# Half of expert 1 for one more pair of sequences, moved from plain matmuls to a paired period

## The chip, the cores and the metric

One NeuronCore of a Trainium2 chip runs the whole program. The time of a run is what the device takes for one execution, in microseconds (us). TensorE (PE) multiplies matrices, VectorE (DVE), ScalarE (ACT) and GpSimd (POOL) do elementwise work, SyncE (SP) issues most DMAs. Each engine works through its own instructions in order and waits on semaphores for the others.

## The reference

Four sequences of 768 tokens with 8 heads of 48 values go through a gated linear attention; the 3072 x 384 result goes through a mixture of eight experts, each of which sees every token; the weights of the experts come from eight rounds of row and column normalization of a gate.

```python
f = 1.0 / (1.0 + np.exp(-f_logit))
for t in range(S):
    state = f[:, :, t, :, None] * state + einsum('bhd,bhe->bhde', k[:, :, t], v[:, :, t])
    y[:, :, t] = einsum('bhd,bhde->bhe', q[:, :, t], state)
x = y as (3072, 384)
P = np.exp(x @ w_gate - max)
for _ in range(8):
    P /= P.sum(1, keepdims=True) + 1e-09; P /= P.sum(0, keepdims=True) + 1e-09; P *= N / E
for e in range(E):                      # w1[e] 384 x 1024, w2[e] 1024 x 384
    out += P[:, e:e + 1] * (np.maximum(x @ w1[e], 0.0) @ w2[e])
```

## The kernel before, in words

Every product is done in 16-bit halves: an operand is split into a high and a low part (xh, xl; w1h, w1l; hh, hl), and three matmuls (high times high, high times low, low times high) stand for one.

**Units and pairs.** A sequence is cut into two halves of 384 tokens, called units u = 0 to 7; b = u // 2 is the pair (one sequence). There are two ways to do an expert for some tokens. The *plain* way computes hidden features and outputs directly: the hidden part goes to a PSUM bank (hps), ScalarE makes its high part with a Relu (hh), VectorE the low part (hl), then output matmuls (yps) follow, and the result is stored to DRAM (yr to ys) to be weighted and added later. The *paired* way works on a whole pair b, on one half m of the 1024 hidden features, with sums of blocks: 15 block products stand for the first matrix product, 7 for the second. One such (e, m, b) is a *period*; ORDER lists the periods.

**Which part is done how.** Experts 0 and 1 are done the plain way (RAW lists their units), experts 2 to 7 the paired way: 6 x 2 x 4 = 48 periods. For the pairs in HALVED the second half of expert 1's features (m = 1) isn't done plain but in one more period each at the end of ORDER. `plain(e, u)` gives the number of 128-feature slices that a plain unit does: 8, or 4 for expert 1 and such a pair.

**The stages.** (1) Attention, up to about 360 us: 24 items of 128 tokens, in a loop of steps (`g`). An item starts every 8 steps and takes its turn in each step with a few instructions of each engine; after the items' turns a step calls `fill(n)`, which takes n units of plain matmuls from the one stream `raw_pairs`. FILL lists n from a step on. One 384-column matmul counts 1 unit, a 128-column one a third. (2) The balancing of the gate (`balance`, L1166 to L1193), a chain of small VectorE and TensorE instructions in 38 steps; a step takes LEAD = 6.9 units of plain work as cover, first what is left of `raw_pairs`, then the last two units of RAW. When `raw_pairs` is used up, `prepare_w1` starts on the first two weight blocks of the paired way. Sums of pairs 2 and 3 are made in the same steps (HASTE). (3) The periods, of 15 slots each. A slot has six matmuls of 256 columns of the period itself, then one or two turns of `paired`, the second product of an earlier period (126 matmuls of 192 columns per period). EVENTS lists what the other engines do, by slot; weights for the period four ahead are prepared at slots listed in W1AT, W2AT and, for the first period, W1AT0 and W2AT0. The matmuls keep the order in which they are written: `mm` makes each depend on the one before.

**Where a plain unit is done how.** Units 0 to 2 (TILED = 3) go through `moe_tile`, 128 tokens at a time: hidden group g = 0 (four slices, 36 matmuls of 128 columns into one bank), its eviction (L467, L470), group 1 and its eviction, then 24 output matmuls of 384 columns. Tiles follow one another in the stream, expert 0 and expert 1 in turn for units 1 and 2. Units 3 to 7 go through `moe`, all 384 tokens at once: per slice nine matmuls of 384 columns and an eviction (L420, L421), then the outputs. The lines of the profile for matmuls are all L312, the line of `mm`.

Of the kernel before, what the change touches and what calls it, by code (L numbers as in the profile page):

```python
# [26 lines left out]
FT = FF // 128  # L27
# [51 lines left out]
END = 27  # L79
W1AT = (0, 1, 2, 3, 5, 9, 10, 11, 12, 21, 23, 25, 26)  # L80
W1AT0 = (16, 18, 19, 19, 22, 23, 23, 27, 27, 33, 35, 40, 41)
W2AT = (4, 22, 25, 25, 27, 29, 30, 35, 38)
W2AT0 = (0, 1, 1, 3, 3, 5, 5, 5, 7)
W2AT1 = (3, 8, 10, 12, 13, 13, 14, 14, 19)
# [7 lines left out]
CONVAT = (3, 6, 7, 9, 11)  # L92
LAST_EVENTS = {18: (('gs', 'C', 1, 1), ('gs', 'C', 1, 2), ('hl', 'C', 1)), 19: (('gs', 'C', 1, 3), ('gf', 'F', 2), ('gh', 1, 0), ('gh', 1, 1))}
ENDING = '.0.1.01.1..12.1.22..23.23.34343444'
HALVED = (2, 3)
ORDER = [(e, m, b) for e in range(2, NE) for m in range(2) for b in range(B)] + [(1, 1, b) for b in HALVED]
PAIRED = (0, 1, 2)
BY_POOL = (1,)
# [9 lines left out]
TS = CT * C  # L108
ONES = CT * NP * D * 4
LEADS = 23  # L110
FILL = ((0, 11.7), (1, 10.3), (2, 0), (3, 0), (5, 2), (6, 0), (7, 6), (8, 6), (9, 0), (10, 6), (12, 5.3), (15, 5.3), (17, 5.3), (23, 8.7), (30, 8.7), (43, 8.0), (195, 7))
LEAD = 6.9
FIRSTAT = ((0,), (0,), (0, 4), (0, 7), (1, 9), (5, 10))
SECONDAT = ((16, 17), (18, 20), (17, 18), (17, 21), (20, 21), (20, 22), (24, 24), (24, 25))
# [169 lines left out]
def fast(ctx, tc, qkf, vbd, wg, w1, w2, out, flag):  # L284
# [10 lines left out]
    def behind(ins, first):  # L295
        tc.add_manual_dep(
            ins.ins, first.ins.name,
            mybir.DependencyInfo(mybir.DependencyClass.NoSync, mybir.DependencyReason.DATA),
            reason="issue order")
# [3 lines left out]
    def pin(ins):  # L303
        engine = ins.ins.engine
        if fixed[0]:
            if engine in last:
                behind(ins, last[engine])
            last[engine] = ins
        return ins

    def mm(transpose=False, **kw):
        ins = (nc.tensor.transpose if transpose else nc.tensor.matmul)(**kw)  # L312
        if order:
            behind(ins, order[-1])
        order.append(ins)
# [20 lines left out]
    for h in range(2):  # L336
        nc.gpsimd.affine_select(
            out=mask[h * 64:(h + 1) * 64], in_=mask[h * 64:(h + 1) * 64],
# [27 lines left out]
    def xof(u):  # L366
        return [x[:, :, u % 2, :] for x in xt[u // 2]]
# [24 lines left out]
    def bank(shape, name):  # L392
        n = banks[0]
        banks[0] += 1
        return (psn if n % 2 and not late else psm).tile(shape, F32, name=name, tag="m")

    def plain(e, u):
        return FT // 2 if e == 1 and u // 2 in HALVED else FT

# [42 lines left out]
    tiles, put_off, owed = [0], [False], []  # L442

    def moe_tile(e, u, t):
        w1s, w2s = ws[e]
        if (u, t) not in ready:
            raise RuntimeError("an expert is ahead of its tokens")
        xh, xl = xof(u)
        ts = slice(t * 128, t * 128 + 128)
        h = []  # L450
        for g in range(2):
            ps = bank([128, 4, 128], f"hps_{e}_{u}_{t}_{g}")
            n = 0
            for q, x in ((0, xh), (0, xl), (1, xh)):
                for f in range(4 * g, 4 * g + 4):
                    a = w1s[f // 2][q]
                    fs = slice((f % 2) * 128, (f % 2) * 128 + 128)
                    for k in range(KT):
                        mm(out=ps[:, f % 4, :], lhsT=a[:, k, fs], rhs=x[:, k, ts], start=(n == 0), stop=(q == 1 and k == KT - 1), skip_group_check=True)
                        n += 1  # L460
                        if n < 36:
                            yield 1 / 3
            i = tiles[0] % FT
            tiles[0] += 1
            th, tl = (hp.tile([128, 2, 256], F16, name=f"h{q}_{e}_{u}_{t}_{g}", tag=f"k{q}{i // 6}{i % 6 // 3}{i % 3}").rearrange("p c t -> p (c t)") for q in "hl")
            pf = ps.rearrange("p f t -> p (f t)")
            pin(nc.scalar.activation(out=th, in_=pf, func=AF.Relu))  # L467

            def low(tl=tl, pf=pf, th=th):
                pin(nc.vector.scalar_tensor_tensor(out=tl, in0=pf, scalar=0.0, in1=th, op0=ALU.max, op1=ALU.subtract))  # L470

            if put_off[0]:
                owed.append(low)
            else:
                low()
            h.append([v.rearrange("p (f t) -> p f t", t=128) for v in (th, tl)])
            yield 1 / 3
        ps = bank([128, DM], f"yps_{e}_{u}_{t}")
        n = 0
        for f in range(FT):  # L480
            if len(owed) > 1 - f // 4:
                raise RuntimeError("a low part is owed")
            wh, wl = w2s[f // 2]
            hh, hl = (v[:, f % 4, :] for v in h[f // 4])
            for a, b in ((hh, wh), (hh, wl), (hl, wh)):
                mm(out=ps, lhsT=a, rhs=b[:, f % 2, :], start=(n == 0), stop=(n == 3 * FT - 1))
                n += 1
                if n < 3 * FT:
                    yield 1
        yr = rp.tile([128, DM], F32, name=f"yr_{e}_{u}_{t}", tag="yraw", bufs=3)  # L490
        pin(nc.scalar.activation(out=yr, in_=ps, func=AF.Copy))
        nc.sync.dma_start(out=yscr[e][u, t * 128:(t + 1) * 128], in_=yr)
        yield 1
# [447 lines left out]
    def raw_pairs(pairs):  # L941
        for e in range(2):
            for t in range(TT):
                yield from moe_tile(e, 0, t)
        for u in range(1, TILED):
            for t in range(TT):
                for e in range(2):
                    yield from moe_tile(e, u, t)
        for e, u in pairs:
            if u >= TILED:  # L950
                yield from moe(e, u, ws[e])
# [3 lines left out]
    def fill(n):  # L955
        credit[0] += n
        while credit[0] > 0.01:
            cost = next(filler, 0)
            if cost == 0:
                return False  # L960
            credit[0] -= cost or 1
        return True
# [12 lines left out]
    def go_all(g):  # L975
        for gen in loads.pop(g, []):
            next(gen, None)
# [141 lines left out]
    live, g = [it, nxt], 0  # L1119
# [6 lines left out]
    while live or g < max(begin):  # L1126
# [14 lines left out]
        put_off[0] = g < PUTOFF  # L1141
        fill([n for at_, n in FILL if g >= at_][-1])
        go_all(g)
# [59 lines left out]
    def prepare_w1(e, j, cuts=(3, 5, 8)):  # L1203
        raw = raw_weights(e, 1, j)
        yield
        sums = kw.tile([128, 10, 128], F32, name=f"k1s_{e}_{j}", tag="sums", bufs=1)

        def block(v):
            if isinstance(v, str):
                q = int(v[1])  # L1210
                return raw[:, q // 2, 128 * (q % 2):128 * (q % 2) + 128]
            return sums[:, WPOS.index(v), :]

        for part in (WSUMS[i:k] for i, k in zip((0,) + cuts, cuts + (None,))):
            for r, p, op, q in part:
                pin(nc.gpsimd.tensor_tensor(out=block(r), in0=block(p), in1=block(q), op=ALU.add if op == '+' else ALU.subtract))  # L1216
            yield
        pin(nc.vector.tensor_reduce(out=wmx[:, 0, 4 * e + j:4 * e + j + 1], in_=raw.rearrange("p a f -> p (a f)"), axis=AX.X, op=ALU.max, apply_absolute_value=True))
        yield
        wh, wl = (kw.tile([128, PRODUCTS, 128], F16, name=f"k1{n}_{e}_{j}", tag=f"k1{n}") for n in "hl")  # L1220
        halves = ((slice(0, 5), sums[:, 0:5]), (slice(5, 10), sums[:, 5:10]))
        ones = ((slice(10, 12), raw[:, 0:2, 0:128]), (slice(12, 15), raw[:, 0:3, 128:256]))
        for parts in (halves[:1], halves[1:], ones):
            for at_, src in parts:
                pin(nc.scalar.activation(out=wh[:, at_, :], in_=src, func=AF.Copy, scale=W1S))
            yield
        for at_, src in halves + ones:
            pin(nc.vector.scalar_tensor_tensor(out=wl[:, at_, :], in0=src, scalar=W1S, in1=wh[:, at_, :], op0=ALU.mult, op1=ALU.subtract))  # L1228
            if src is ones[1][1]:
                k1[e, j] = wh, wl  # L1230
            yield
# [233 lines left out]
    def at_all(n, slots, gen):  # L1465
        for slot in slots:
            at_slots(n + slot // PRODUCTS, (slot % PRODUCTS,), gen)

    for n, (e, m, b) in enumerate(ORDER):
        part = n % 4  # L1470
        if n - part + 4 < PERIODS and part in (0, 2):
            e2, m2, _ = ORDER[n - part + 4]
            gen = prepare_w1(e2, 2 * m2 + part // 2)
            at_all(n, W1AT if n else W1AT0, gen)
        if n == 0:
# [214 lines left out]
```

## Time and profile before

| | |
|---|---|
| median of 3 runs | 1459.27 us (1458.95 to 1459.32) |
| profiled execution | 1458.97 us, span 1457.2 us |
| TensorE busy | 1435.4 us (99%), 16188 matmuls |
| weight loads | 1267.0 us (87%) |
| VectorE busy | 1241.6 us (85%) |
| ScalarE busy | 1112.2 us (76%) |
| POOL busy | 1092.3 us (75%) |
| granted TensorE clock, mean | 0.997 |

Busy times are unions of an engine's instructions in the profile. A matmul's row runs from its start to the modelled end of its result, which overlaps the next one's row, so the pace of TensorE is read from starts, not from durations. A bracket at the end of a row is the idle time before the instruction and who ended it.

### The profile page before, as it was taken

To read this page: it belongs to the slowest core of one execution; us is meant where nothing else is said; L and a number is where in the kernel's file an instruction comes from. 1 tells how busy PE (TensorE), PEld (TensorE's weight loads), DVE (VectorE), ACT (ScalarE), POOL (GpSimd) and SP (SyncE) were. 2 spreads that over 40 slices of the span, in tenths; PEclk is the share of its full clock that TensorE was granted. 3 is DMA by queue.
4 is the path that set the end of the run, shared out by engine and by line. 5 is a ranking of instruction groups with operands and counts; after the bars stand their busy time and mean duration, and the time that the engine had idled before them with its cause. 6 is when DMAs were issued, how large, how long until landed. Compare 5 with 4: busy or idle time off the path is not lost.

```text
span 1457.2 us, 40795 instructions
## 1 busy us (share of the span) xinstructions
PE 1435.4 (99%) x16188; PEld 1267.0 (87%) x16188; DVE 1241.6 (85%) x2540; ACT 1112.2 (76%) x2492; POOL 1092.3 (75%) x1288
## 2 busy tenths in 40 slices
PE   7999999999999999999999999999999999999997
PEld 5788886666568899999999999999999999999997
DVE  8868878877868998888899898888888889888886
ACT  7767778875547778888888888888777787778874
POOL 3244665675625769999999999999888888888874
PEclk9999999999999999999999999999999999999999
DMA  9245544541111011222211111111000000000201
GB/s 265 84 113 132 120 110 126 124 120 47 65 49 35 24 40 47 56 62 61 61 55 58 49 50 45 41 51 49 23 23 24 23 23 23 13 15 20 77 13 69
DMA packets 82955, 90.54 MB, mean 62 GB/s; under 512 B 50017, under 2 KB 69601, under 8 KB 82754
## 3 DMA queue, kind: packets, MB, share of 16 engines
q1 hardware_dynamic: 82322, 87.25, 21.6%
q8 instruction: 128, 2.10, 0.6%
q14 instruction: 73, 0.60, 0.1%
q10 hardware_dynamic: 432, 0.59, 0.1%
HBM read 64.03 MB, written 14.16 MB: 54 GB/s over the span
## 4 chain that ended last, share of the span: by engine, by line
PE 73%; DVE 3%; ACT 1%; POOL 0%; issue 0%; ACTq 0%; POOLq 0%; DVEq 0%
PE kyps L312 29%; PE kb_A L312 9%; PE kb_B L312 8%; PE kb_D L312 6%; PE kxps L312 5%; PE kb_C L312 4%; PE yps L312 4%; PE hps L312 3%; PE kb_E L312 2%; PE kb_F L312 2%; DVE k1l L1228 0%; DVE kf L1538 0%; DVE kl L1569 0%; POOL k1s L1216 0%; DVE acc L1387 0%
## 5 line engine op out<-in xcount | busy, mean ns | idle before, releaser
L312 PEld LDWEIGHTS <-k1h 128*128 128x128 f16 x3000 | 282.5, 98 | 21.4 <-issue 1.1
L312 PE MATMUL kyps<-k2h,kgl 128*128 128x192 f16 x1188 | 292.3, 246 | 0.6 <-POOL kgl L1564 0.6
L312 PE MATMUL kyps<-k2h,kgh 128*128 128x192 f16 x1188 | 292.3, 246 | 0.1
L312 PE MATMUL kyps<-k2l,kgh 128*128 128x192 f16 x1188 | 292.2, 246 | 0.0
L312 PEld LDWEIGHTS <-kgh 128*128 128x128 f16 x2400 | 220.9, 98 | 7.2 <-issue 0.5
L1564 POOL TENSOR_TENSOR kgl<-kf,kgh 128x512 f16<-128x512 f32 x148 | 198.4, 1341 | 2.1 <-ACT kgh L1561 2.1
L1387 DVE SCALAR_TENSOR_TENSOR yy<-kyps,pes,part 128x192 f32<-128x192 f32 x270 | 111.5, 413 | 92.5 <-PE kyps L312 82.3
L1564 POOL TENSOR_TENSOR kgl<-kr,kgh 128x512 f16<-128x512 f32 x148 | 175.4, 1185 | 9.1 <-PE kyps L312 7.7
L1430 POOL TENSOR_TENSOR acc<-acc,yy 128x384 f32<-128x384 f32 x135 | 134.9, 1000 | 58.4 <-DVE yy L1387 58.4
L312 PEld LDWEIGHTS <-k1l 128*128 128x128 f16 x1500 | 146.8, 98 | 16.9
L312 PEld LDWEIGHTS <-kh 128*128 128x128 f16 x1200 | 112.6, 98 | 7.9 <-issue 1.3
L312 PEld LDWEIGHTS <-kgl 128*128 128x128 f16 x1200 | 117.4, 98 | 0.9 <-POOL kgl L1564 0.8
L312 PEld LDWEIGHTS <-w1h 128*128 128x128 f16 x1248 | 87.9, 98 | 27.1 <-issue 2.1
L312 PE MATMUL yps<-w2h,hl 128*128 128x384 f16 x336 | 110.1, 328 | 1.0 <-DVE hl L470 0.9
L312 PE MATMUL yps<-w2l,hh 128*128 128x384 f16 x336 | 110.0, 328 | 0.6 <-DVE w2l L385 0.6
L312 PE MATMUL yps<-w2h,hh 128*128 128x384 f16 x336 | 110.1, 328 | 0.2 <-ACT hh L420 0.2
L1515 ACT ACTIVATE cp<-kb_A 128x512 f32<-128x512 f32 x150 | 89.8, 599 | 17.5 <-DVE kb_A L1517 15.9
L1541 POOL TENSOR_TENSOR kr<-kr 128x256 f32<-128x256 f32 x100 | 75.6, 756 | 33.5 <-DVE xbl L1029 26.4
L312 PEld LDWEIGHTS <-hh 128*128 128x128 f16 x672 | 65.1, 99 | 37.2 <-issue 1.0
L1384 ACT ACTIVATE kyps<-kyps 128x192 f32<-128x192 f32 x148 | 47.7, 322 | 65.2 <-PE kyps L312 65.1
L1561 ACT ACTIVATE kgh<-kf 128x512 f16<-128x512 f32 x150 | 94.9, 633 | 1.7 <-DVE kf L1538 1.6
L1561 ACT ACTIVATE kgh<-kr 128x512 f16<-128x512 f32 x150 | 94.3, 629 | 0.6 <-DVE kr L1538 0.6
(323 smaller groups left out, 5383.6 us busy)
## 6 DMA issues: line engine op xcount, KB each, us to landing
q<-in_qkf_dram SPq DMA_DIRECT2D x23, 672.0 KB, 5.0
k1r<-in_w_dram SPq DMA_DIRECT2D x26, 384.0 KB, 3.0
k2r<-in_w_dram SPq DMA_DIRECT2D x26, 384.0 KB, 3.0
ys<-yr SPq DMA_DIRECT2D x48, 192.0 KB, 2.4
yb<-ys SPq DMA_DIRECT2D x48, 192.0 KB, 2.4
vr<-in_vbd_dram SPq DMA_DIRECT2D x24, 192.0 KB, 2.5
out_dram<-acc SPq DMA_DIRECT2D x21, 192.0 KB, 1.9
w1r<-in_w_dram SPq DMA_DIRECT2D x8, 384.0 KB, 9.4
```

What stands on the lines that cost most here:

```text
L312: ins = (nc.tensor.transpose if transpose else nc.tensor.matmul)(**kw)
L1384: pin(nc.scalar.activation(out=out, in_=in_, func=AF.Copy, **kw))
L1387: pin(nc.vector.scalar_tensor_tensor(out=y, in0=ps, scalar=p, in1=z, op0=ALU.mult, op1=ALU.add))
L1430: pin(nc.gpsimd.tensor_tensor(out=y, in0=y, in1=z.rearrange("p s d -> p (s d)"), op=ALU.add))
L1515: pin(nc.scalar.activation(out=fresh(ev[2]), in_=bk, func=AF.Copy))
L1541: pin((nc.gpsimd if ev[2] == 'P' else nc.vector).tensor_tensor(out=r[:, 0], in0=r[:, 1], in1=r[:, 0], op=ALU.subtract))
L1561: pin(nc.scalar.activation(out=hs['g', t][0][i], in_=hs['f' if i else 'r', t], func=AF.Copy))
L1564: pin((nc.vector if tag == str(PERIODS - 1) and ev[1] else nc.gpsimd).tensor_tensor(out=hs['g', t][1][i], in0=hs['f' if i else 'r', t], in ...
```

## The change

HALVED becomes (1, 2, 3): for pair 1, too, the second half of expert 1's features is no longer done in the plain units (1, 2) and (1, 3) but in a period (1, 1, 1), the first of the last group; there are 51 periods instead of 50. `moe_tile`, through which unit (1, 2) goes, now honours `plain(e, u)`: a tile with four slices has one hidden group and 12 output matmuls. FILL hands out 0.3 units less per attention step from step 23 on, and 1.0 less from step 195. Six of the thirteen slots in W1AT0 become earlier ones. Since `first` and `final` follow from ORDER, the output of pair 1 is stored in the new period.

```diff
-W1AT0 = (16, 18, 19, 19, 22, 23, 23, 27, 27, 33, 35, 40, 41)
+W1AT0 = (16, 18, 19, 19, 22, 23, 23, 25, 26, 26, 29, 37, 40)
...
-HALVED = (2, 3)
+HALVED = (1, 2, 3)
 ORDER = [(e, m, b) for e in range(2, NE) for m in range(2) for b in range(B)] + [(1, 1, b) for b in HALVED]
...
-FILL = (..., (17, 5.3), (23, 8.7), (30, 8.7), (43, 8.0), (195, 7))
+FILL = (..., (17, 5.3), (23, 8.4), (43, 7.7), (195, 6.0))
...
         h = []
-        for g in range(2):
+        fts = plain(e, u)
+        for g in range(fts // 4):
             ps = bank([128, 4, 128], f"hps_{e}_{u}_{t}_{g}")
...
-        for f in range(FT):
-            if len(owed) > 1 - f // 4:
+        for f in range(fts):
+            if len(owed) > fts // 4 - 1 - f // 4:
                 raise RuntimeError("a low part is owed")
...
-                mm(out=ps, lhsT=a, rhs=b[:, f % 2, :], start=(n == 0), stop=(n == 3 * FT - 1))
+                mm(out=ps, lhsT=a, rhs=b[:, f % 2, :], start=(n == 0), stop=(n == 3 * fts - 1))
                 n += 1
-                if n < 3 * FT:
+                if n < 3 * fts:
                     yield 1
```

## Rows read from the trace of the kernel before

**Rows 1.** Stretches: each engine's busy us (instructions), granted clock, DMA
```profile
100.00:350.00 250.00, 249.42 (x3621) 188.00 (x3620) 200.60 (x384) 189.63 (x409) 146.17 (x158) 1.00 0.46 114
260.00:280.00 20.00, 19.69 (x286) 13.99 (x284) 18.85 (x35) 16.37 (x37) 11.03 (x13) 1.00 0.58 149
361.00:410.00 49.00, 48.17 (x304) 29.28 (x301) 42.14 (x93) 23.45 (x48) 33.24 (x51) 1.00 0.21 68
380.00:400.00 20.00, 19.47 (x124) 11.74 (x122) 19.09 (x42) 11.48 (x25) 14.58 (x21) 1.00 0.08 30
410.00:425.00 15.00, 15.00 (x95) 8.98 (x92) 5.43 (x10) 6.19 (x12) 0.00 (x0) 1.00 0.12 40
425.00:505.00 80.00, 78.61 (x766) 69.68 (x765) 68.88 (x138) 59.11 (x133) 46.67 (x62) 1.00 0.11 33
560.00:1380.00 820.00, 819.94 (x8759) 778.46 (x8757) 723.54 (x1513) 664.52 (x1528) 732.59 (x856) 1.00 0.14 40
```

**Rows 2.** TensorE in order of time, 86 to 90 us: start, duration, operation
```profile
86.46 0.33 PE L312 MATMUL yps<-w2h,hh 128*128 128x384 f16 x1
86.62 0.33 PE L312 MATMUL yps<-w2l,hh 128*128 128x384 f16 x1
...
89.56 0.34 PE L312 MATMUL yps<-w2h,hl 128*128 128x384 f16 x1 [0.66 <-DVE hl L470]
```

**Rows 3.** All engines in order of time, 186 to 190 us
```profile
186.12 0.83 PE L312 MATMUL hps<-xh,w1h 128*128 128x128 f16 x12
...
187.10 0.60 ACT L467 ACTIVATE hh<-hps 128x512 f16<-128x512 f32 x1
...
187.73 0.69 DVE L470 SCALAR_TENSOR_TENSOR hl<-hps,hh 128x512 f16<-128x512 f32 x1 [1.50 <-ACT hh L467]
...
188.13 0.33 PE L312 MATMUL yps<-w2h,hh 128*128 128x384 f16 x1
...
188.33 0.60 ACT L467 ACTIVATE hh<-hps 128x512 f16<-128x512 f32 x1
...
189.20 0.68 DVE L470 SCALAR_TENSOR_TENSOR hl<-hps,hh 128x512 f16<-128x512 f32 x1
```

**Rows 4.** Tile kb_F, 560 to 1380 us: durations, first and last start
```profile
L1520 DVE TENSOR_TENSOR kb_F<-kb_D,cp x40: 698/699/700, 579.7 to 1368.2; 128x512 f32<-128x512 f32 x40
```

**Rows 5.** All engines in order of time, 137 to 138 us
```profile
137.03 0.33 PE L312 MATMUL yps<-w2h,hh 128*128 128x384 f16 x1
...
137.22 0.60 ACT L467 ACTIVATE hh<-hps 128x512 f16<-128x512 f32 x1 [0.46 <-PE hps L312]
...
137.85 0.69 DVE L470 SCALAR_TENSOR_TENSOR hl<-hps,hh 128x512 f16<-128x512 f32 x1 [1.05 <-ACT hh L467]
```

**Rows 6.** All engines in order of time, 197 to 200 us
```profile
197.64 0.33 PE L312 MATMUL yps<-w2h,hh 128*128 128x384 f16 x1
...
198.96 0.60 ACT L467 ACTIVATE hh<-hps 128x512 f16<-128x512 f32 x1
...
199.11 0.32 PE L312 MATMUL yps<-w2l,hh 128*128 128x384 f16 x1
...
199.59 0.69 DVE L470 SCALAR_TENSOR_TENSOR hl<-hps,hh 128x512 f16<-128x512 f32 x1 [2.03 <-ACT hh L467]
```

**Rows 7.** VectorE in order of time, 86 to 90 us
```profile
88.84 0.66 DVE L470 SCALAR_TENSOR_TENSOR hl<-hps,hh 128x512 f16<-128x512 f32 x1
```

**Rows 8.** VectorE's groups, 410 to 425 us: busy, mean ns, idle before
```profile
L421 DVE SCALAR_TENSOR_TENSOR hl<-hps,hh 128x384 f16<-128x384 f32 x7 | 3.9, 557 | 7.5 <-ACT hh L420 7.4
```

**Rows 9.** All engines in order of time, 393 to 395 us
```profile
394.06 0.30 PEld L312 LDWEIGHTS sk_c<-sk_cs,onesf 128*128 128x128 f32 x2 [0.84 <-DVE sk_cs L1188]
...
394.09 0.72 POOL L1005 TENSOR_TENSOR xs<-x 128x256 f32<-128x256 f32 x1
```

**Rows 10.** VectorE's groups of instructions, 100 to 350 us
```profile
L1029 DVE TENSOR_TENSOR xal<-xs,xah 128x768 f16<-128x768 f32 x3 | 2.9, 951 | 0.0
```

**Rows 11.** VectorE's groups of instructions, 355 to 425 us
```profile
L1029 DVE TENSOR_TENSOR xal<-xs,xah 128x768 f16<-128x768 f32 x6 | 6.9, 1146 | 0.0
```

More of the change, by code (lines that the diff above doesn't have):

```diff
@@ L110 @@
 LEADS = 23
-FILL = ((0, 11.7), (1, 10.3), (2, 0), (3, 0), (5, 2), (6, 0), (7, 6), (8, 6), (9, 0), (10, 6), (12, 5.3), (15, 5.3), (17, 5.3), (23, 8.7), (30, 8.7), (43, 8.0), (195, 7))
+FILL = ((0, 11.7), (1, 10.3), (2, 0), (3, 0), (5, 2), (6, 0), (7, 6), (8, 6), (9, 0), (10, 6), (12, 5.3), (15, 5.3), (17, 5.3), (23, 8.4), (43, 7.7), (195, 6.0))
 LEAD = 6.9
```

## The prediction, made before the changed kernel was built or run

> **What bounds the kernel now.** I read the busy times of each engine by stretch first [rows 1]. TensorE is busy 249.42 of 250 us while attention runs, 48.17 of 49 around the balancing, 819.94 of 820 in the steady part of the paired periods, and the granted clock is 1.00 (2.4 GHz) in all of them. Since overlapping matmuls make a busy TensorE easy to overrate, I checked that it is at its pace: in the list of instructions two output matmuls of 384 columns start 0.16 us apart (86.46 and 86.62, 0.162 over longer runs), and a hidden group of 36 matmuls of 128 columns takes the 2.01 us from 186.12 to 188.13, 0.056 each [rows 2, 3]. So from 100 us on nearly every microsecond of matmul taken away or added counts, and so does every wait on TensorE. VectorE is the next engine: 200.6 of 250 us, 42.1 of 49 [rows 1].
>
> **What goes.** Units (1,2) and (1,3), expert 1 on the two halves of sequence pair 1, lose half of their hidden features. Unit (1,2) is done in 128-token tiles: per tile 36 matmuls of 128 columns and 12 of 384 go, for three tiles 108 x 0.056 + 36 x 0.162 = 11.9 us. Unit (1,3) is done whole: 4 x 9 + 3 x 12 = 72 of 384 columns, 11.7 us. Together 23.6 us, or 144 of the "units" that FILL counts (a unit is one 384-column matmul or three of 128). Seven evictions on ScalarE and seven on VectorE go too; no output store goes.
>
> **What comes.** One more period, (1,1,1): 90 matmuls of 256 columns and 126 of 192. Its length is read from one event per period: 40 of them start between 579.7 and 1368.2 us, 788.5 / 39 = 20.22 us [rows 4]. Weights for (1,1) are prepared for the last group anyway, so it brings no loads, and VectorE, busy 88% in the steady periods with such loads beside [rows 1], has room. The output of pair 1 is stored three periods later, still two periods ahead of the end. Matmul work alone: 20.22 - 23.6 = -3.4 us.
>
> **The step that I think decides: the half tile has nothing to hide its eviction.** A full tile computes hidden group 0, then group 1, then the outputs, which begin with group 0. Group 0's high part (ScalarE) and low part (VectorE) are made beside group 1's 36 matmuls (2.0 us), and group 1's beside the first 12 output matmuls (1.95 us). A half tile has one group: its first output matmul needs the high part and its third the low part at once. Nothing else stands between, since the tiles follow one another in one stream and TensorE keeps the written order.
>
> How long the two parts take, counted from where the next matmul could start: in a quiet tile the next one starts at 137.03, the high part ends at 137.82 and the low part at 138.54: 0.79 and 1.51 us [rows 5]. Behind other work it is 197.64, 199.56 and 200.28: 1.92 and 2.64 [rows 6]; at 186.12 (still hidden of group 1 next) 1.58 and 2.30, and at 188.13 0.80 and 1.75 [rows 3]. One tile shows the wait itself. Its group 1 ends at 86.46 and the low part at 89.50, 3.04 later [rows 7]; the fifteenth output matmul, which needs it, would be due 14 x 0.162 = 2.27 us after 86.46, at 88.73, and starts at 89.56 [rows 2]. So TensorE starts 0.06 after the low part ends and loses what is over. For the half tile the third matmul would be due after 2 x 0.162 = 0.32 us, so a tile loses (low part's end) + 0.06 - 0.32: at least 1.25 us (from 1.51), at most 2.78 (from 3.04).
>
> Which value, from the place in the attention schedule: FILL's new amounts hand out 106.3 units before step 23, 168 in the next 20 steps, then 7.7 a step. The three half tiles finish their hidden part at units 636, 708 and 780, which is late in step 89, early in step 99 and past the middle of step 108. An item starts every 8 steps and issues its score and state matmuls in steps that are 3 above a multiple of 8, its output matmuls in 1, its gate in 7. Step 90 issues none, and 99 and 108 end later than the tile's third matmul, so none of the three waits is covered by attention matmuls (as the one after 197.64 is, whose next output matmul comes at 199.11 in any case [rows 6]). Step 89 has the second scan and the products before it on VectorE: between 1.51 and 2.30, I take 1.9. Step 99 is of the kind of the 186.12 tile but a little earlier in its step: 2.5. Step 108 is of the kind of 188.13 (1.75), 2.5 units or 0.4 us earlier: 2.1. Sum 6.5 - 3 x 0.26 = 5.7 us lost; ends 3.75 and 8.3.
>
> **The smaller terms.** Unit (1,3) and the other half units have this only mildly, since four evictions are spread over 36 matmuls and the last one's low part is due only 11 x 0.162 = 1.78 us later: nothing is lost behind a quiet VectorE (1.51), 0.9 with 2.64. I take 0.2.
> Attention steps get 0.3 units shorter (the last ones 1.0), 65.6 units or 10.7 us in all. VectorE then has about the same work in 240 us for 250, 84% for 80%. In the 20 us from 260 it already has 18.85, and TensorE idles 0.31 there [rows 1]. Nothing lost at the one end, five such stretches at the other, 1.5; I take 0.2.
> The balancing of the gate is 38 steps long and takes 6.9 units a step as cover. Left over for it are 1728 - 1594.3 = 133.7 units before and 1584 - 1528.7 = 55.3 after, plus 216 of the last two units in both: 349.7 or 271.3, against 38 x 6.9 = 262. So the cover still reaches, with little over. But the first two weight blocks, which are prepared once the earlier units are used up, then begin at step 9 instead of 20 and are done before the balancing ends: VectorE gets the 1.5 us of their low parts that now lie after 410 (5.43 us of work there [rows 1], less 3.9 of hidden low parts [rows 8]), and two hidden evictions more (1.1 us), 44.7 for 42.1 us in a stretch of 49 [rows 1]. There TensorE's queue already waits 0.84 us for VectorE's column sums at 394.06 [rows 9]. If VectorE can be 95% busy, as in 380 to 400 (19.09 of 20), nothing is lost; if no more than its 86% there, 44.7 / 0.86 - 49 = 3.0 us. I take 1.2, between the two.
> W1AT0 moves six of the thirteen pieces of one weight block's preparation (ScalarE's and VectorE's splitting) forward by one to seven slots within periods 1 and 2, where they queue ahead of other evictions; nothing waits for them before period 4; 80 us from 425 hold 78.61 of TensorE [rows 1], so at most 1.4 either way, taken as 0.
>
> **The sum.** -3.4 + 5.7 + 0.2 + 0.2 + 1.2 = +3.9 us on the profiled execution's own 1458.97 (span 1457.2 and 1.8 around it), 1462.9; the median of the timed runs lies 0.3 higher, so 1463.2.
>
> One rule speaks against the change in its balancing part. VectorE's low parts of pair sums take 0.95 us while attention runs and 1.15 beside the denser POOL work there [rows 10, 11], 0.2 more each. The Trainium skill, SBUF — State Buffer (Who interferes with whom), says that a VectorE instruction with two SBUF inputs and a POOL instruction that reads SBUF lock each other out for a whole instruction. By the rows the eight low parts of weights that come to lie beside POOL's sums cost VectorE 8 x 0.2 = 1.6 us; by the rule up to a whole POOL sum each, 8 x 0.72 = 5.8 us (the sum at 394.09 [rows 9]). The rows bear out a part of the rule only; all of it would be rival 3.
>
> **The rivals.**
> 1. The half tiles' waits are covered after all: not slower. Place: the three points at units 636, 708, 780; it decides if each falls right before a step with attention matmuls, which take 1.3 us or more (between the output matmuls at 197.64 and 199.11 [rows 6]), or if TensorE's order differs from the written one. Then -3.4 + 1.6 of smaller terms at most, at least 0.3: 1456.2 to 1457.5, 1456.3 with little elsewhere. Against it stands the count of steps, and the wait at 89.56, where later matmuls didn't go ahead. Chance 0.08.
> 2. The waits stay at their floor and the rest costs next to nothing: -3.4 + 3.75 + 0.3 = +0.7, 1460.0. For it: a stalled TensorE lets VectorE catch up, and two of the five evictions read were nearly quiet ones. Chance 0.30, with all else that ends within 0.2%.
> 3. Balancing starves: VectorE late by 3 to 6 us in a stretch with 1.3 steps of spare cover, so that column sums and evictions are waited for. -3.4 + 5.7 + 0.4 + 4 = +6.7, 1466.0. For it: the wait at 394.06 [rows 9]; against: POOL and ScalarE have room there (33.2 and 23.5 of 49 us [rows 1]), so VectorE alone would have to be late. Chance 0.15.
> The forecast has the remaining 0.47.
>
> **How the numbers follow.** 0.2% is 2.9 us, about what a measurement of this kernel tells from no change. The forecast (0.47) and rival 3 (0.15) give slower 0.62, rival 2 same 0.30, rival 1 faster 0.08. The range leaves out rival 1 and the case that all three open terms stand at their upper ends: 1457.8 to 1467.2. The likeliest case's own range is 1461 to 1466.
>
> **What would show it.** In the changed profile: three gaps before 384-column output matmuls between about 150 and 205 us, each in two pieces (for the high part, then for the low part), 1.3 to 2.8 us together, where now there is none. Attention's end about 5 us earlier (10.7 less the waits). Balancing about 12.7 us shorter, with more waits for column sums. 51 periods of 20.22 us. Wrong, if the half tiles run without gaps, or if waits in the balancing or in periods 0 to 3 outweigh theirs.

## The result, and the profile after

The changed kernel takes 1467.03 us (median of six runs, 1466.78 to 1468.52), the kernel before in the same call 1459.11 (1458.87 to 1459.32): a ratio of 1.0057 [1.0044, 1.0070], 7.9 us slower where 3.9 was forecast. The direction is right, and the time still lies inside the range, at its upper edge; the loss is twice the forecast one. The profiled spans differ by the same 7.9 us (1465.1 against 1457.2).

Events that both kernels have show where it went.

| event | before | after | moved |
|---|---|---|---|
| last gate matmul (lps) starts | 360.9 | 358.1 | -2.8 |
| first matmul of a period (kb_A) starts | 425.5 | 414.7 | -10.8 |
| sixth kb_F starts | 539.3 | 527.4 | -11.9 |
| last kb_F starts | 1429.9 | 1437.9 | +8.0 |

The instructions of these tiles over the whole span after, each with count, shortest, median and longest duration in ns, first and last start:

```profile
L312 PE MATMUL lps<-wgs,xl x72: 169/169/170, 38.9 to 358.1; 128*128 128x16 f16 x72
...
L312 PE MATMUL kb_A<-xbh,k1h x306: 269/273/273, 414.7 to 1431.0; 128*128 128x256 f16 x153
...
L1521 DVE TENSOR_TENSOR kb_F<-kb_D,cp x51: 699/699/700, 427.8 to 1437.9; 128x512 f32<-128x512 f32 x51
```

The count of kb_F is 51, 50 before: the added period is there. Attention hands out 65.6 units or 10.7 us less matmul work and ends 2.8 earlier (about 5 was forecast), so 7.9 us of it came back as waits. Balancing, from the last gate to the first period, went from 64.6 to 56.6 us: 8.0 shorter where 12.7 us of work are gone, so 4.7 came back. Up to the sixth kb_F another 1.1 us was gained. The periods keep their pace, so the added one costs its 20 us.

The stretches after, in the columns of [rows 1]:

```profile
100.00:350.00 250.00, 244.13 (x3512) 181.88 (x3509) 201.06 (x385) 191.51 (x413) 147.09 (x158) 1.00 0.45 116
380.00:400.00 20.00, 15.36 (x95) 8.95 (x94) 18.36 (x36) 7.67 (x17) 17.04 (x25) 1.00 0.09 30
425.00:505.00 80.00, 79.41 (x809) 72.83 (x808) 70.56 (x148) 61.44 (x139) 56.75 (x78) 1.00 0.12 36
560.00:1380.00 820.00, 819.95 (x8761) 778.51 (x8759) 724.26 (x1510) 662.00 (x1521) 730.07 (x853) 1.00 0.13 40
```

TensorE idles 5.9 us of the 250 of attention (0.6 before) and 4.6 of the 20 around 390 (0.5 before), at an unchanged clock of 1.00. VectorE's busy time in those 20 us, 18.36, is even below the 19.09 of before: its share doesn't tell that TensorE waits for it.

**The half tiles.** The three gaps are where they were expected, in two pieces each. All engines in order of time around them (the bracket is the idle time before the instruction and who ended it):

```profile
166.40 0.60 ACT L468 ACTIVATE hh<-hps 128x512 f16<-128x512 f32 x1 [2.76 <-PE hps L312]
166.60 1.21 DVE L752 TENSOR_TENSOR_SCAN q<-ft,pib 112x512 f32<-112x512 f32 x1
167.05 0.34 PE L312 MATMUL yps<-w2h,hh 128*128 128x384 f16 x1 [0.69 <-ACT hh L468]
...
167.73 0.67 DVE L471 SCALAR_TENSOR_TENSOR hl<-hps,hh 128x512 f16<-128x512 f32 x1
...
168.45 0.34 PE L312 MATMUL yps<-w2h,hl 128*128 128x384 f16 x1 [0.90 <-DVE hl L471]
...
185.89 0.34 PE L312 MATMUL yps<-w2h,hh 128*128 128x384 f16 x1 [1.53 <-ACT hh L468]
...
186.61 0.34 PE L312 MATMUL yps<-w2h,hl 128*128 128x384 f16 x1 [0.23 <-DVE hl L471]
...
201.89 0.34 PE L312 MATMUL yps<-w2h,hh 128*128 128x384 f16 x1 [0.69 <-ACT hh L468]
...
202.62 0.34 PE L312 MATMUL yps<-w2h,hl 128*128 128x384 f16 x1 [0.23 <-DVE hl L471]
```

Two matmuls of 384 columns start 0.16 us apart at pace, and a row overlaps the next by as much, so each loss is the bracket and 0.16 more: 0.85 + 1.06, 1.69 + 0.39, 0.85 + 0.39, together 5.2 us where 5.7 was taken. In the first tile the low part had to wait for the scan in VectorE's order, as the kind of step 89 suggested.

**The rest of attention.** Two more places, again in order of time:

```profile
288.55 0.34 PE L312 MATMUL yps<-w2h,hl 128*128 128x384 f16 x1 [0.33 <-DVE hl L421]
...
290.07 1.21 DVE L752 TENSOR_TENSOR_SCAN q<-ft,pib 112x512 f32<-112x512 f32 x1
...
291.20 0.53 DVE L421 SCALAR_TENSOR_TENSOR hl<-hps,hh 128x384 f16<-128x384 f32 x1
...
291.79 0.34 PE L312 MATMUL yps<-w2h,hl 128*128 128x384 f16 x1 [1.28 <-DVE hl L421]
...
349.39 0.95 DVE L992 TENSOR_TENSOR x<-xh,xl 128x768 f32<-128x768 f16 x1
350.26 1.54 DVE L830 SCALAR_TENSOR_TENSOR sl<-st,sh 48x384 f16<-48x384 f32 x2
...
351.86 0.41 PE L312 MATMUL yps<-qh,sl 112*128 112x64 f16 x8 [1.29 <-DVE sl L830]
```

A half unit's last low part stands behind a scan; the state's low part (sl) stands behind a pair sum (x). TensorE loses 0.5, 1.4 and 1.5 us, 3.4 where the kernel before had 1.1 us of such waits. With the half tiles' 5.2 that makes 7.5 of the 7.9 us; the remaining 0.4 is not placed.

**The balancing.** VectorE, and at the end TensorE's instruction that waits for it, in order of time:

```profile
381.25 1.18 DVE L1030 TENSOR_TENSOR xal<-xs,xah 128x768 f16<-128x768 f32 x1
...
384.05 1.02 DVE L1229 SCALAR_TENSOR_TENSOR k1l<-k1s,k1h 128x640 f16<-128x640 f32 x1
384.99 1.48 DVE L1030 TENSOR_TENSOR xal<-xs,xah 128x768 f16<-128x768 f32 x1
...
387.49 0.76 DVE L1229 SCALAR_TENSOR_TENSOR k1l<-k1s,k1h 128x640 f16<-128x640 f32 x1
...
388.55 0.37 DVE L1189 TENSOR_REDUCE sk_cs<-pe 128x8 f32<-128x200 f32 x1
...
388.97 0.39 PE L312 MATMUL sk_c<-sk_cs,onesf 128*128 128x8 f32 x2 [2.79 <-DVE sk_cs L1189]
```

The column sum (sk_cs) that the chain needs next comes after the low parts of two pair sums (xal) and two low parts of one weight block (k1l); the steps of the chain itself, left out here, lie between them. One of the xal takes 1.48 us, where they took 0.95 on average in attention and 1.15 here before [rows 10, 11]. TensorE, out of cover for this step, waits 2.8 us for it. By the waits of 358 to 416 us (total, times, longest) there are two of these:

```profile
PE sk_c L312 <- DVE sk_cs L1189: 4.5, 2, 2.8
```

and in the kernel before, 355 to 425 us, one:

```profile
PE sk_c L312 <- DVE sk_cs L1188: 0.5, 1, 0.5
```

### The profile page after: what moved, and what is told of

It is laid out like the page before. It is cut to its first block, busy times and chain, and to the rows that moved or that the text cites. A ratio compares the mean times of both kernels' runs of the same rounds, so it can differ in the third digit from the quotient of the medians.

```text
span 1465.1 us, 40868 instructions
## 1 busy us (share of the span) xinstructions
PE 1433.4 (98%) x16188; PEld 1269.7 (87%) x16188; DVE 1254.4 (86%) x2565; ACT 1123.0 (77%) x2518; POOL 1107.7 (76%) x1301
## 4 chain that ended last, share of the span: by engine, by line
PE 80%; DVE 5%; ACT 1%; issue 1%; ACTq 0%; DVEq 0%
PE kyps L312 30%; PE kb_A L312 9%; PE kb_B L312 9%; PE kb_D L312 7%; PE yps L312 5%; PE kxps L312 5%; PE kb_C L312 5%; PE hps L312 4%; PE kb_E L312 2%; PE kb_F L312 2%; DVE hl L421 1%; PE aps L312 0%; DVE sl L830 0%; PE kvb L312 0%; ACT hh L420 0%
## 5 line engine op out<-in xcount | busy, mean ns | idle before, releaser
L312 PEld LDWEIGHTS <-k1h 128*128 128x128 f16 x3060 | 288.0, 98 | 21.1 <-issue 0.9
L312 PE MATMUL kyps<-k2h,kgh 128*128 128x192 f16 x1212 | 298.1, 246 | 0.1
L312 PE MATMUL kyps<-k2h,kgl 128*128 128x192 f16 x1212 | 298.1, 246 | 0.0
L312 PE MATMUL kyps<-k2l,kgh 128*128 128x192 f16 x1212 | 298.1, 246 | 0.0
L312 PEld LDWEIGHTS <-kgh 128*128 128x128 f16 x2448 | 225.3, 98 | 7.3 <-issue 0.5
L312 PE MATMUL yps<-w2h,hl 128*128 128x384 f16 x312 | 102.3, 328 | 3.2 <-DVE hl L421 1.6
L312 PE MATMUL yps<-w2h,hh 128*128 128x384 f16 x312 | 102.3, 328 | 2.9 <-ACT hh L468 2.9
L312 PE MATMUL yps<-w2l,hh 128*128 128x384 f16 x312 | 102.2, 328 | 0.6 <-DVE w2l L385 0.6
L312 PEld LDWEIGHTS <-w1h 128*128 128x128 f16 x1152 | 80.9, 98 | 25.0 <-issue 2.1
L312 PEld LDWEIGHTS <-hh 128*128 128x128 f16 x624 | 59.7, 98 | 37.1 <-ACT hh L468 3.4
```

## The experiments

Three places are to be explained: half tiles, the rest of attention, balancing; and there is a gain in the first periods. Each experiment undoes or does one of them. Ratios are to the kernel before, run in the same call (medians 1459.20 to 1459.32).

**1. Hidden parts of both experts first.** The changed kernel, but in unit (1, 2) expert 1's hidden part of a tile comes before the output matmuls of expert 0's tile, so that these hide its eviction.

```diff
-    for e in range(2):
-        yield from moe_tile(e, u, t)
+    h = []
+    for e in range(2):
+        h.append((yield from hidden(e, u, t)))     # moe_tile cut in two
+    for e in range(2):
+        yield from moe_tile(e, u, t, h[e])         # the output part
```

> The changed kernel, but for unit 2 the hidden part of the expert 1 tile is computed before the output matmuls of the expert 0 tile, so 24 output matmuls (3.9 us) lie between a half tile's eviction and its use. Theory (the half tiles wait for their own eviction): the six waits between 166 and 203 us, 5.2 us together in the changed kernel's trace, go, and the time falls by 5.2 us to about 1461.8, 1460.5 to 1463 as the later evictions shift a little. Rival (VectorE is the bound of this stretch, so the lateness turns up elsewhere): waits of about the same sum between 160 and 358 us and over 1465.5.

Measured: 1461.82 us (1461.26 to 1463.18), 1.0019 [1.0010, 1.0029]. That is 2.6 above before where the changed kernel is 7.9 above: 5.3 us back, of 5.2 read from the gaps. TensorE's waits in attention (100 to 354 us) no longer hold a half tile, and the other two lines stand as in the changed kernel:

```profile
PE yps L312 <- DVE hl L421: 1.6, 2, 1.3
...
PE yps L312 <- DVE sl L836: 1.3, 1, 1.3
```

No work was removed, only the order changed, so the order is the cause, and nothing late came up behind it.

**2. Weights later.** The changed kernel, with the first two weight blocks of the periods begun no earlier than step 14 of the balancing.

```diff
-        if kw is not None and not prepared:
+        if kw is not None and not prepared and step >= 14:
```

> The changed kernel, but the first two weight blocks are started at balancing step 14 instead of 9. Theory (their reduction and low parts on VectorE stand in front of the column sums): the two long waits for column sums (2.8 and 1.9 us) become at most half, 2 to 3 us are won, about 1464.5. Rival (the balancing is simply too short for what VectorE has to do in it, whatever the order): waits of the same sum, later, within 1 us of the changed kernel, 1466 to 1468.

Measured: 1464.35 us (1464.02 to 1464.39), 1.0035 [1.0022, 1.0047]: 2.8 us back. The waits for column sums, 358 to 413 us:

```profile
PE sk_c L312 <- DVE sk_cs L1189: 1.6, 3, 1.0
```

The same eight low parts are made in the same balancing, only later: 2.8 of the 4.7 us hung on that. With them the edit moves the rest of the preparation, two reductions on VectorE, the high parts on ScalarE and the sums on POOL; which of these the 2.8 us hang on was not separated. About 1.9 us stay.

**3. Old slots.** The changed kernel with the old W1AT0.

```diff
-W1AT0 = (16, 18, 19, 19, 22, 23, 23, 25, 26, 26, 29, 37, 40)
+W1AT0 = (16, 18, 19, 19, 22, 23, 23, 27, 27, 33, 35, 40, 41)
```

> The changed kernel with the old slots of W1AT0. Theory (the new slots took the waits of 0.4 to 0.8 us at 476 to 489 us of the kernel before away): they come back in periods 1 to 3 and it is about 1.1 us slower, 1468.1. Rival (those waits went because the periods start with other work behind them): within 0.3 us of the changed kernel.

Measured: 1468.14 us (1467.82 to 1469.81), 1.0065 [1.0048, 1.0082]. The new slots are worth about 1.0 us. Experiment 5 does the opposite: the new W1AT0 alone in the kernel before.

> The kernel before with only the new slots of W1AT0. Theory (the new slots by themselves take away the waits of 0.79, 0.40 and 0.70 us between 476 and 489 us): 1.1 us faster than before, 1458.1. Rival (they help only where the periods start as in the changed kernel): within 0.3 us of before.

Measured: 1458.01 us (1457.45 to 1458.39), 0.9991 [0.9982, 1.0001]: 1.3 us, at the edge of what the interval tells, but of the size of experiment 3 with the sign turned. The waits agree. TensorE in the kernel before, 425 to 505 us:

```profile
PE kyps L312 <- POOL kgl L1564: 0.6, 1, 0.6
...
PE kb_A L312 <- ACT cp L1515: 0.5, 1, 0.5
...
PE kb_B L312 <- DVE kl L1569: 0.2, 1, 0.2
```

and with the new slots alone, same stretch, one of the three is left:

```profile
PE kb_A L312 <- ACT cp L1515: 0.6, 1, 0.6
```

**4. The new FILL alone,** in the kernel before. No work is removed: 65.6 units of plain work come later (not 78, as the expectation has it).

```diff
-FILL = (..., (23, 8.7), (30, 8.7), (43, 8.0), (195, 7))
+FILL = (..., (23, 8.4), (43, 7.7), (195, 6.0))
```

> The kernel before with only the new, smaller FILL; all plain units as before, 78 units more left for the balancing. Theory (shorter attention steps alone do little; it is where a short unit's evictions fall that costs): waits in the attention stretch within 1 us of before, the time 1458.5 to 1460.5. Rival (the shorter steps make VectorE late everywhere): waits of 2.5 us or more beyond those of before between 100 and 358 us, 1461.5 or more.

Measured: 1462.06 us (1461.84 to 1462.31), 1.0020 [1.0010, 1.0029]. The theory had missed: 2.9 us for shorter steps alone, the rival's time, though not quite its waits. Attention ends 8.5 us earlier where 10.7 us of work left it, so about 2.1 us are new waits there, against the rival's 2.5; the other 0.9 lies in the balancing. A part of the 2.1 lies before 100 us, where a wait for kvb grows from 0.3 to 1.3 us and one of 0.7 for hl goes. TensorE's waits in attention, 100 to 353 us:

```profile
PE yps L312 <- DVE sl L829: 0.8, 2, 0.5
PE yps L312 <- DVE hl L421: 0.6, 2, 0.4
```

VectorE in order of time ahead of the first of them, the 0.5 us for sl at 230.35:

```profile
228.71 0.56 DVE L421 SCALAR_TENSOR_TENSOR hl<-hps,hh 128x384 f16<-128x384 f32 x1 [2.21 <-ACT hh L420]
229.19 1.11 DVE L829 SCALAR_TENSOR_TENSOR sl<-st,sh 48x384 f16<-48x384 f32 x2
```

VectorE is idle for 2.21 us while sl, whose operands are at hand, stands behind a low part that waits for ScalarE. At this place that isn't an engine with too much work; it is an order that fitted longer steps. The wait of 0.2 us for hl at 265.01 is of another kind: from 258.67 on VectorE has no break there. Experiment 7 tries to take work off it.

**6. Experiments 1 and 2 together.**

> The changed kernel with both edits: the half tiles' hidden parts ahead of the expert 0 tile's output matmuls, and the first weight blocks from balancing step 14. Theory (two separate costs): both gains add, 5.2 + 2.7 below the changed kernel, 1459.1. Rival (with the attention over sooner, VectorE enters the balancing with more behind it, and part of the gain is lost there): 1460.5 or more.

Measured: 1458.75 us (1458.33 to 1458.96), 0.9997 [0.9988, 1.0007]: 8.5 us back, and 5.3 + 2.8 are 8.1. The two gains add up.

**7. Less work for VectorE.** Experiment 4 with the pair sums (x = xh + xl) of pairs 0 and 1, six additions in attention, on POOL instead of VectorE.

```diff
-X_BY_POOL = ()
+X_BY_POOL = (0, 1)
```

> The kernel before with the new FILL (1462.1 by itself), and the six additions with which the pair sums of pairs 0 and 1 begin (0.95 us each on VectorE during attention) given to POOL, which is busy under 60% there. Theory (VectorE's amount of work makes it late in the shorter steps): the waits for sl and hl between 225 and 320 us, 2.1 us, shrink by half or more, 1460.5 to 1461. Rival (it is the order and place of the scans and evictions, not the amount): 1461.8 or more.

Measured: 1465.24 us (1465.19 to 1465.31), 1.0041 [1.0027, 1.0056]: 3.1 us slower than experiment 4. By the events 2.0 of them arise up to the first period, and about 1.2 in the periods around 950 us, where no cause was looked for. TensorE's longest waits, 100 to 360 us:

```profile
PE yps L312 <- DVE sl L829: 1.8, 3, 0.9
PE yps L312 <- DVE hl L470: 0.6, 1, 0.6
```

Six instructions fewer on VectorE, and the waits for it grew. But its work did not shrink. The group of all sl on VectorE, 100 to 350 us (busy us, mean ns), in experiment 4,

```profile
L829 DVE SCALAR_TENSOR_TENSOR sl<-st,sh 48x384 f16<-48x384 f32 (+1 forms) x38 | 31.3, 823 | 4.2 <-ACT sh L821 3.6
```

and in experiment 7:

```profile
L829 DVE SCALAR_TENSOR_TENSOR sl<-st,sh 48x384 f16<-48x384 f32 (+1 forms) x38 | 36.4, 958 | 4.2 <-ACT sh L821 3.6
```

Of VectorE's additions 5.8 us went (9.3 to 3.5), but its sl take 5.1 us longer and its product q 1.1 (12.7 to 13.8): they are slower beside POOL's work, as the last section shows, and two of the waits for sl (0.9 and 0.6 us, at 232.21 and 258.72) follow such slowed ones. In the kernel POOL's pair sums of that step are made to wait until sl is done; the additions given to POOL have no such tie. So the run shows that this move doesn't help. It doesn't test whether VectorE's amount of work makes attention late, and no other run separates amount from order there.

**8. The same at one place.** Experiment 6, with only pair 2's sums on POOL, the ones in front of the sl at 350.26.

```diff
-X_BY_POOL = ()
+X_BY_POOL = (2,)
```

> As e6, and the three additions of pair 2 in the last attention steps (0.95 us each, right ahead of the sl that TensorE waits 1.46 us for at the end of the attention) given to POOL. Theory (that sl is late because of the addition in front of it): the wait goes and it is 1.2 to 1.5 us faster than e6, about 1457.8, under the kernel before. Rival (POOL is late in its place and holds up the pair sums and then ScalarE): no faster than e6.

Measured: 1457.10 us (1456.94 to 1457.52), 0.9985 [0.9976, 0.9995], 1.6 us below experiment 6. The sl wait of 1.5 us is gone. Here, too, the last two sl run beside an addition on POOL and take 1.47 us together, but with no addition in front of them they end in time.

**9. Half units slice by slice.** Experiment 8, and in half units of 384 tokens the output matmuls go through the three token tiles for slices 0 and 1, then for slice 2, then for slice 3, instead of one token tile with all slices after another. The last slice's high part is then needed after 27 output matmuls instead of 9, and its low part, which the expectation's 27 is meant for, after 29 instead of 11.

```diff
-        for t in range(TT):
-            ps = bank([128, DM], f"yps_{e}_{u}_{t}")
-            for f in range(fts):
+        turns = [(t, r) for r in (range(2), range(2, 3), range(3, 4)) for t in range(TT)]
+        for t, fr in turns:                        # one bank per t; half units only
+            for f in fr:
```

> As e8, and the output matmuls of the half units of 384 tokens go slice by slice over the three token tiles (slices 0 and 1 for all tiles, then 2, then 3), so the last slice's low part is due after 27 matmuls (4.4 us) instead of 11. Theory (a half unit has too few matmuls between its last evictions and their use): the waits of 0.51 and 1.43 us go, 1.9 us faster than e8, about 1455.2. Rival (three PSUM banks are held at once, and the next unit's hidden part waits for a bank): no faster than e8.

Measured: 1455.68 us (1455.27 to 1455.90), 0.9976 [0.9967, 0.9986]: 3.5 us below before and, over it, 11.4 below the changed kernel. It beats both. It brought 1.3 us of the 1.9 expected, since a smaller wait came up at 263 us. TensorE's waits in attention of experiment 8, 100 to 352 us,

```profile
PE yps L312 <- DVE hl L421: 1.6, 2, 1.3
```

and of experiment 9, 100 to 350 us:

```profile
PE yps L312 <- DVE hl L421: 0.2, 1, 0.2
```

**10. Low parts of pair sums apart.** Experiment 9 with the low parts of pair 2's sums in every second step of the balancing.

```diff
-HASTE = (..., (2, "HL", 14, 45, 1, 1), ...)
+HASTE = (..., (2, "HL", 14, 45, 2, 1), ...)
```

> As e9, and the splitting of pair 2's sums is handed out every second balancing step instead of every step. Theory (VectorE's low parts of the sums, 1.2 to 1.5 us each beside POOL, stand in front of the column sums): the waits of 1.1 and 0.6 us shrink by 1 us or more, about 1454.2. Rival (VectorE has the same work in the same steps, and the waits move later): within 0.5 us of e9.

Measured: 1457.17 us (1456.90 to 1458.32), 0.9987 [0.9978, 0.9997]: 1.5 slower than experiment 9, the theory fell. The waits for column sums were 1.5 us in three pieces in experiment 9; here one of them alone costs more, all engines in order of time:

```profile
394.69 0.74 ACT L1243 ACTIVATE k1h<-k1s 128x640 f16<-128x640 f32 x1 [2.32 <-POOL k1s L1234]
...
395.83 0.56 DVE L421 SCALAR_TENSOR_TENSOR hl<-hps,hh 128x384 f16<-128x384 f32 x1 [2.38 <-ACT hh L420]
...
396.31 0.20 DVE L1210 RECIPROCAL sk_cs<-sk_c 128x8 f32<-128x8 f32 x1
...
399.54 0.39 PE L312 MATMUL sk_c<-sk_cs,onesf 128*128 128x8 f32 x2 [2.20 <-DVE sk_cs L1206]
```

It isn't the pair sums that stand in front of this column sum; the last of their low parts ended at 392.98. The chain's next step (the reciprocal) stands on VectorE behind a hidden low part, for which VectorE idles 2.38 us; that one waits for its high part, which stands on ScalarE behind the high part of a weight block, and this waits for the block's sums on POOL. Those ended at 392.5 in experiment 9 and at 394.7 here. So the spacing moved the second weight block's sums later, and a chain over three engines' orders carried it to TensorE. (The profiled execution took 1458.24 us, 1.1 above the median; TensorE's clock fell behind this wait, see the last section.) What makes up the 1.9 us that experiment 2 left in the balancing is not settled by this.

## Why the prediction came out too low

- **Matmul work, -3.4:** right. The added period costs 20 us, and experiments 1, 2 and 6 come out within 0.7 us of what is left when waits are taken off.
- **The half tile has nothing to hide its eviction, +5.7:** right in mechanism, place and size (5.2 by the gaps, 5.3 by experiment 1). Tile by tile 1.6, 2.2 and 1.8 had been taken and 1.9, 2.1 and 1.2 came, so a little of the closeness is luck. The floor of 3.75 in rival 2 and the cover of rival 1 are refuted.
- **Balancing, +1.2 with ends 0 and 3.0:** this is the step that failed. It measured 4.7, above its own upper end. The cause was named rightly, weights prepared some ten steps earlier on VectorE (2.8 us by experiment 2). The price was not: it was reckoned as an amount of work over a share of busy time. VectorE was busy 18.36 of 20 us, within the 95% called free there, and TensorE still lost 4.6 us in that stretch. By the rows of the wait at 388.97 and by experiment 2, what counts is which low parts stand in front of a column sum in VectorE's order at the moment when a step's cover has run out. How much of it is that order and how much the slower low parts beside POOL was not separated, and 1.9 of the 4.7 us stay unexplained. Rival 3 had the size (4) and the right sign, with 0.15.
- **Half units and shorter attention steps, +0.2 and +0.2:** 2.7 measured (7.9 of waits less 5.2). This term failed in the same way: the bounds 0.9 and 1.5 were read, both were then taken near zero, and 2.7 lies above even their sum of 2.4 (the wait at 291.79 alone is 1.4). Experiment 4 puts shorter steps alone at 2.1 us in attention. One wait there shows why (VectorE idle for 2.21 us with sl ready behind): the written order of VectorE was made for longer steps. That this holds for the other waits, and not VectorE's amount of work, is not shown.
- **W1AT0, 0 with 1.4 either way:** -1.1 by the events, -1.0 and -1.3 by experiments 3 and 5, inside the bounds.

With what was measured in place of the terms: -3.4 + 5.2 + 2.7 + 4.7 - 1.1 = +8.1, against 7.9. The 2.7 and 4.7 are what the events leave over, so this is bookkeeping; the tests of the terms are experiments 1 to 5. The forecast's +3.9 lacks 3.5 in the balancing and 2.3 in attention, and had 0.5 too much in the half tiles and no gain from W1AT0.

## What to carry to other kernels

Where engines run a written order, price an edit by what stands in front of each awaited instruction, on every engine of the chain, and not by an engine's share of busy time alone: 2.8 us went by starting the preparation of two weight blocks later, and in experiment 10 2.2 us came from one weight block's sums that were late on POOL. Work given to another engine isn't gone either: check what it slows down there (experiment 7). When work that served as cover is removed, walk through the order once more, since every place in it was chosen for the old distances; halving a producer's groups needs another group between its eviction and its use (experiments 1 and 9). And when several small unknowns all have the same sign, take their middles rather than their lower ends; here that alone would have brought the forecast from 3.9 to 5.0 only.

## What the chip showed that was not expected

**A sum on POOL.** Two of the six additions on POOL (tile x) in experiment 7, VectorE and POOL in order of time,

```profile
229.54 1.64 POOL L991 TENSOR_TENSOR x<-xh,xl 128x768 f32<-128x768 f16 x1
...
230.62 1.54 DVE L829 SCALAR_TENSOR_TENSOR sl<-st,sh 48x384 f16<-48x384 f32 x2
...
255.80 2.86 DVE L829 SCALAR_TENSOR_TENSOR sl<-st,sh 48x384 f16<-48x384 f32 x2
256.04 1.64 POOL L991 TENSOR_TENSOR x<-xh,xl 128x768 f32<-128x768 f16 x1
```

and the sl of the second place in experiment 4, without the addition:

```profile
254.53 1.26 DVE L829 SCALAR_TENSOR_TENSOR sl<-st,sh 48x384 f16<-48x384 f32 x2
```

The addition takes 1.64 us on POOL where VectorE's row after has 0.95. The first two sl beside it take 1.54 us, 1.11 without (the row of experiment 4); they overlap for 0.56 us, from 230.62 to 231.18, and 0.43 of that is lost. At the second place the whole addition falls into the two sl, and they take 1.60 us longer. The Trainium skill, SBUF — State Buffer (Who interferes with whom), says that such a pair, a VectorE instruction with two SBUF inputs and a POOL instruction that reads SBUF, contend; the trace agrees, with most of the overlap lost, and nearly the whole POOL instruction where all of it overlaps, as in the prediction's upper price. In the balancing less was lost: the xal of 1.48 us is 0.53 over the 0.95 of [rows 10].

**The clock after a long wait.** TensorE's granted clock fell behind some waits of over 2 us and not behind others. Stretches of experiment 1 behind a wait that ends at 383.62 us:

```profile
380.00:384.00 4.00, 1.22 (x9) 0.67 (x7) 3.93 (x8) 0.00 (x0) 1.26 (x4) 0.98 0.00 0
384.00:388.00 4.00, 4.00 (x17) 1.94 (x15) 3.97 (x7) 1.10 (x3) 3.76 (x6) 0.59 0.13 49
```

and of the changed kernel behind the wait that ends at 388.97:

```profile
388.00:392.00 4.00, 3.03 (x20) 1.92 (x21) 3.97 (x8) 1.10 (x3) 3.38 (x6) 1.00 0.13 49
```

In experiment 1 it was granted 0.59 on average over 4 us, near the lower of its two levels (1.2 of 2.4 GHz); in the changed kernel it stayed at 1.00 behind a wait of the same length. In experiment 3, the same kernel up to there, it fell behind that very wait (0.57 over 389 to 393 us), so it differs between executions of the same instructions. Where it fell it cost nothing in the end: VectorE caught up meanwhile, and the second wait for a column sum, 1.9 us in the changed kernel, shrank to 0.2. In experiment 10 the fall after the wait that ends at 399.54 us (0.60 over 400 to 404 us) had no such wait behind it. What decides whether it falls was not tried.
